# Cross-covariance attention and highway layer: outputs of one batch beside the scores of the next, in a fixed order

## The chip, the core and the metric

The kernel runs on one core of one Trainium2 chip. The metric is the device time of one execution in microseconds (us). Engines: PE multiplies matrices, ACT (ScalarE) applies functions, DVE (VectorE) and POOL (GpSimd) work element by element, SP (SyncE) issues stores; loads that change the type are issued by POOL. Matmul results lie in PSUM, eight banks of 512 f32 per partition, everything else in SBUF.

## What is computed

```python
def _attn_ref(q, k, v, tau):                     # q, k, v: (4, 6336, 256) f32, tau = 1
    qn = q / (np.linalg.norm(q, axis=1, keepdims=True) + 1e-06)
    kn = k / (np.linalg.norm(k, axis=1, keepdims=True) + 1e-06)
    s = kn.transpose(0, 2, 1) @ qn / tau         # 256 x 256 for each batch
    s = s - s.max(-1, keepdims=True)
    a = np.exp(s)
    a /= a.sum(-1, keepdims=True) + 1e-09
    return (v @ a).astype(np.float32)

def _moe_ref(x, w_h, w_t, b_t):                  # x: the 25344 rows of the above
    H = np.maximum(x @ w_h, 0.0)
    T = 1.0 / (1.0 + np.exp(-(x @ w_t + b_t)))
    return (T * H + (1.0 - T) * x).astype(np.float32)
```

## The kernel before

A batch has 6336 rows, 50 tiles of 128 rows (the last has 64). q, k and v are loaded in groups of 16 tiles, cast from f32 to f16 on the way, one row of 256 elements to a partition and tile (`_load_group`, L399 for whole groups, L406 for the short last one). For each of four batches:

- *Scores* (L129, L136, L143): for every tile six matmuls add up k'q and the diagonal blocks of k'k and q'q in two PSUM tiles `sg`. All tiles of a batch must be in before anything is known of the softmax.
- *Chain* (L151 to L248): copies of `sg`, norms from the diagonals, square root on ACT (L172), reciprocal, scaling (L193), exponential (L202), row sums (L204), the attention matrix in f16 in `mr`, its transpose, and its products with w_h and w_t (`ahat`, L241), which are put beside it. `mr` is then the 256 x 768 right side [a | a w_h | a w_t].
- *Outputs*, in pairs of tiles: PE transposes v (L284) into the bank `vtps`; every fourth pair is copied to SBUF by DVE (L296), the others by ACT (L301). Then come the gate matmuls `p3b` (L329) with the bias added by a further matmul (L343), and `p3a` (L336), 512 columns that hold x and x w_h. ACT takes the sigmoid `tt` (L354), DVE max(h, 0) t in `th` (L365) and (t - 1) x in `ux` (L373), a tile at a time, and POOL subtracts (L381). SP stores eight tiles at once (L416).

Loads of the next batch's q and k, and of its first v group, are issued by POOL after the chain (L251), v's other groups from the output loop (L272). Four buffers each hold q and k, three v. The order on each engine is made by the framework's scheduler from this program; it may take PE's work of the next batch forward where its inputs allow. A load waits on a semaphore until its buffer is free; the program has eight semaphores for POOL's loads, used in turn (DMASW0 to DMASW7 in the rows below), and a load that takes one waits until the load that used it last has landed.

## Time and profile before

| | us |
|---|---|
| median of three runs (lowest, highest) | 385.34 (384.37, 387.27) |
| the profiled execution | 384.06 |
| its span | 382.2 |
| PE, DVE, ACT, POOL busy | 296.3, 172.4, 133.2, 186.1 |
| loads in DMA queue 0, share of 16 engines | 76.3% |
| stores in DMA queue 1, share of 16 engines | 22.3% |
| longest pieces of the chain by kind: PE, DMA | 42%, 39% |

The span is the time from the first to the last instruction of the profiled execution. Busy time is summed over it, so an engine that is idle in one stretch and full in the next shows a middling share. GB/s counts bytes as written: a load reads twice as many as it writes. "Idle before <-X" says which work the engine waited for. In the chain, each step is followed back to what released it.

### The profile page before, as it was taken

The numbers are of one execution on the slowest core, as the hardware profiler recorded it, in microseconds if no ns is written. First come the engines' busy times: TensorE is split into PE (matmuls) and PEld (weight loads), VectorE is DVE, ScalarE is ACT, GpSimd is POOL, SyncE is SP. The second block draws the span as 40 slices with busy tenths as digits, with TensorE's granted clock in tenths as the row PEclk, the third lists the DMA queues.
The fourth block names the chain that finished last, engine by engine and source line by source line (L and its number), as shares of the span: only waits on it lengthen the run. The fifth ranks groups of instructions, "written<-read, shape, count | busy, mean of one in ns | idle before, by whom it ended". The sixth has DMA issues, their size and how long they took to land.

```text
span 382.2 us, 6609 instructions
## 1 busy us (share of the span) xinstructions
PE 296.3 (78%) x2637; PEld 211.6 (55%) x2637; DVE 172.4 (45%) x498; ACT 133.2 (35%) x231; POOL 186.1 (49%) x173
## 2 busy tenths in 40 slices
...
GB/s 90 196 198 199 197 198 199 198 210 223 110 157 111 195 237 199 198 198 197 239 250 103 111 163 217 212 200 138 216 231 111 203 237 24 0 101 131 128 194 140
DMA packets 103455, 65.56 MB, mean 172 GB/s; under 512 B 1537, under 2 KB 103425, under 8 KB 103425
## 3 DMA queue, kind: packets, MB, share of 16 engines
q0 software_dynamic: 77568, 39.20, 76.3%
q1 hardware_dynamic: 25856, 25.95, 22.3%
q8 instruction: 20, 0.33, 0.3%
...
## 4 chain that ended last, share of the span: by engine, by line
PE 42%; DMA 39%; DVE 5%; ACT 4%; POOL 4%; issue 3%; POOLq 0%; DVEq 0%; ACTq 0%
DMA k<-in_k_dram 21%; PE p3a L336 19%; DMA v<-in_v_dram 14%; PE p3b L329 8%; DMA q<-in_q_dram 5%; PE p3b L343 4%; PE vtps L284 4%; PE sg L129 3%; ACT tt L354 3%; DVE th L365 2%; DVE ux L373 2%; PE sg L136 2%; PE sg L143 2%; POOL q L399 1%; POOL o L381 1%
## 5 line engine op out<-in xcount | busy, mean ns | idle before, releaser
L381 POOL TENSOR_TENSOR o<-th,ux 128x512 f32<-128x512 f32 (+1 forms) x104 | 128.7, 1246 | 111.1 <-DVE ux L373 93.6
L336 PE MATMUL p3a<-mr,vtsb 128*128 128x512 f16 (+1 forms) x400 | 126.3, 386 | 1.0
L129 PE MATMUL sg<-q,k 128*128 128x256 f16 (+1 forms) x400 | 96.0, 283 | 37.7 <-DMA k<-in_k_dram 35.1
L365 DVE SCALAR_TENSOR_TENSOR th<-p3a,tt 128x256 f32<-128x256 f32 x200 | 84.1, 421 | 41.1 <-ACT tt L354 24.6
L354 ACT ACTIVATE tt<-p3b 128x512 f32<-128x512 f32 (+1 forms) x104 | 60.3, 581 | 101.5 <-PE p3b L343 87.8
L136 PE MATMUL sg<-k 128*128 128x128 f16 (+1 forms) x400 | 90.4, 226 | 0.0
L143 PE MATMUL sg<-q 128*128 128x128 f16 (+1 forms) x400 | 90.2, 226 | 0.0
L329 PE MATMUL p3b<-mr,vtsb 128*128 128x256 f16 (+1 forms) x400 | 87.0, 276 | 0.5 <-ACT tt L354 0.3
L373 DVE SCALAR_TENSOR_TENSOR ux<-tt,p3a 128x256 f32<-128x256 f32 x200 | 82.1, 410 | 0.0
L296 DVE CAST vtsb<-vtps 128x512 f16<-128x512 f32 (+1 forms) x28 | 18.2, 651 | 123.9 <-PE vtps L284 103.7
L284 PE MATMUL vtps<-ident,v 128*128 128x128 f16 (+1 forms) x400 | 45.2, 225 | 29.7 <-DMA v<-in_v_dram 25.4
L129 PEld LDWEIGHTS <-k 128*128 128x128 f16 (+1 forms) x400 | 40.6, 101 | 42.5 <-DMA k<-in_k_dram 41.2
L284 PEld LDWEIGHTS <-v 128*128 128x128 f16 (+1 forms) x400 | 32.4, 101 | 46.9 <-DMA v<-in_v_dram 26.2
L343 PE MATMUL p3b<-btb,ident 128*128 128x256 f16 x200 | 55.3, 277 | 0.0
L301 ACT CAST vtsb<-vtps 128x512 f16<-128x512 f32 (+1 forms) x76 | 43.1, 567 | 33.9 <-PE vtps L284 31.8
L329 PEld LDWEIGHTS <-vtsb 128*128 128x128 f16 (+1 forms) x400 | 38.1, 100 | 22.8 <-issue 2.5
L336 PEld LDWEIGHTS <-vtsb 128*128 128x128 f16 (+1 forms) x400 | 37.5, 99 | 20.0 <-issue 6.3
L143 PEld LDWEIGHTS <-q 128*128 128x128 f16 (+1 forms) x400 | 40.6, 102 | 6.7 <-issue 0.6
L136 PEld LDWEIGHTS <-k 128*128 128x128 f16 (+1 forms) x400 | 40.6, 101 | 1.3 <-issue 0.7
L153 ACT COPY ssb<-sg 128x512 f32<-128x512 f32 x8 | 4.3, 589 | 84.4 <-PE sg L143 84.4
L399 POOL DMA_DIRECT2D k<-in_k_dram x12 | 14.0, 1163 | 27.2 <-PE sg L143 23.5
L343 PEld LDWEIGHTS <-ident 128*128 128x128 f16 x200 | 19.8, 99 | 13.0 <-issue 2.0
...
## 6 DMA issues: line engine op xcount, KB each, us to landing
...
```

What stands on the lines that cost most here:

```text
L129: nc.tensor.matmul(sg[c][:, 0:C], kt_[0:nr, si, bass.ts(c, P)], qt[0:nr, si, :], start=first, stop=False,)
L136: nc.tensor.matmul(sg[c][:, C : C + P], kt_[0:nr, si, bass.ts(c, P)], kt_[0:nr, si, bass.ts(c, P)], start=False, stop=False,)
L143: nc.tensor.matmul(sg[c][:, C + P : C + 2 * P], qt[0:nr, si, bass.ts(c, P)], qt[0:nr, si, bass.ts(c, P)], start=False, stop=last,)
L284: nc.tensor.matmul(vtps[:, u, c, 0:nr], vt_in[0:nr, si + u, bass.ts(c, P)], ident[0:nr, 0:nr], start=(pcnt == 0), stop=(pcnt == 2 * pn - 1),)
L301: nc.scalar.copy(out=vt_sb[:, 0:pn, :, 0 : nrows[0]], in_=vtps[:, 0:pn, :, 0 : nrows[0]],)
L329: nc.tensor.matmul(p3b[0:nr, u, :], vt_sb[:, u, kt, 0:nr], mr[:, kt, 2 * C : 3 * C], start=(kt == 0 and u == 0), stop=False,)
L336: nc.tensor.matmul(pa[0:nr, :], vt_sb[:, u, kt, 0:nr], mr[:, kt, 0 : 2 * C], start=(kt == 0), stop=(kt == 1),)
L343: nc.tensor.matmul(p3b[0:nr, u, :], ident[:, 0:nr], btb, start=False, stop=(u == pn - 1),)
L354: nc.scalar.activation(out=tt[0:nr0, 0:pn, :], in_=p3b[0:nr0, 0:pn, :], func=Act.Sigmoid,)
L365: nc.vector.scalar_tensor_tensor(out=th[0:nr, u, :], in0=p3a[u][0:nr, C : 2 * C], scalar=0.0, in1=tt[0:nr, u, :], op0=AluOp.max, op1=AluOp ...
L373: nc.vector.scalar_tensor_tensor(out=ux[0:nr, u, :], in0=tt[0:nr, u, :], scalar=1.0, in1=p3a[u][0:nr, 0:C], op0=AluOp.subtract, op1=AluOp. ...
L381: nc.gpsimd.tensor_tensor(out=ostg[0:nr0, si : si + pn, :], in0=th[0:nr0, 0:pn, :], in1=ux[0:nr0, 0:pn, :], op=AluOp.subtract,)
```

## The change

The body is written anew for an order that is fixed by the program's text (`manual_schedule`).

- A partition now takes 49 consecutive rows of a batch, so that each load and store moves one contiguous piece per partition; the 64 rows left over are a tile of their own. q and k come in five groups of 12, 12, 12, 9 and 4 tiles with six buffers, v in groups of 16, 16 and 17 with four.
- All scores of batch 0 stand first, then its chain. After that the work goes in 100 slots of two row tiles: gate matmuls, transposes for the slot three ahead, h and x matmuls, the elementwise operations, and as many score tiles of the next batch as `P1_END` says (50 in slots 0 to 17, 50 in 18 to 42, 50 in 43 to 67, none after). The chain of the next batch is spread over seven slots.
- The bias matmuls go; ACT writes the bias into a gate bank two slots ahead (L379), and the gate matmuls add to it.
- `th` and `ux` are formed for two tiles at once (512 elements per partition). h and x of a slot have a bank each out of three (`hx`); the chain's matmuls use the same three. The transposes have one bank (`vT`), emptied by ACT for even and by DVE for odd tiles.
- The square root moves from ACT to POOL as a power, the row sums into the exponential.
- Buffers of loads are refilled from within the slots, one slot after they come free.

The core of the diff; what it removes is the body printed above.

```diff
+    QG = [(0, 12), (12, 12), (24, 12), (36, 9), (45, 4)]
+    NQG = len(QG)
+    QRING = 6
...
+    VG = [(0, 16), (16, 16), (32, 17)]
...
+    VRING = 4
...
+    LOOK = 3
+    P1_END = [18, 43, 68]
...
+    ctx.enter_context(tc.manual_schedule())
...
+    def rows(src2d):
+        return src2d[0:NF, :].rearrange("(p s) c -> p s c", s=NS)
...
+    def load_qk(n):
+        b, g = divmod(n, NQG)
...
+        s0, ns = QG[g]
+        q_t[n] = stream_pool.tile([P, 12, C], f16, tag="q_in", bufs=QRING, name=f"q{n}")
+        k_t[n] = stream_pool.tile([P, 12, C], f16, tag="k_in", bufs=QRING, name=f"k{n}")
+        nc.gpsimd.dma_start(out=q_t[n][:, 0:ns, :], in_=rows(q[b])[:, s0 : s0 + ns, :])
+        nc.gpsimd.dma_start(out=k_t[n][:, 0:ns, :], in_=rows(k[b])[:, s0 : s0 + ns, :])
+        if g == 0:
+            qr_t[b] = stream_pool.tile([P, C], f16, tag="q_rem", bufs=2, name=f"qr{b}")
+            kr_t[b] = stream_pool.tile([P, C], f16, tag="k_rem", bufs=2, name=f"kr{b}")
+            nc.gpsimd.dma_start(out=qr_t[b][0:REM, :], in_=q[b][NF:N, :])
+            nc.gpsimd.dma_start(out=kr_t[b][0:REM, :], in_=k[b][NF:N, :])
...
+    def load_v(m):
...
+        v_t[m] = stream_pool.tile([P, 18, C], f16, tag="v_in", bufs=VRING, name=f"v{m}")
+        nc.gpsimd.dma_start(out=v_t[m][:, 0:ns, :], in_=rows(v[b])[:, s0 : s0 + ns, :])
+        if g == NVG - 1:
+            nc.gpsimd.dma_start(out=v_t[m][0:REM, ns, :], in_=v[b][NF:N, :])
...
+    for n in range(NQG):
+        load_qk(n)
...
-    nc.gpsimd.dma_start(out=bt_sb, in_=moe_b_t.rearrange("(a m) -> a m", a=1))
...
-    btb = const_pool.tile([P, C], f16, tag="btb")
-    nc.scalar.copy(out=btb, in_=btp)
...
+    load_v(0)
+    load_qk(NQG)
...
+    nc.sync.dma_start(out=bt_sb, in_=moe_b_t.rearrange("(a m) -> a m", a=1))
...
+    make_identity(nc, ident0)
...
+    nc.vector.tensor_copy(out=ident, in_=ident0)
+    ones32 = const_pool.tile([P, P], f32, tag="ones32")
+    nc.vector.memset(ones32, 1.0)
...
+    load_v(1)
+    load_v(2)
...
+    def hx_tile(name):
+        return psum_pool.tile([P, 2, C], f32, tag="hx", bufs=3, name=name)
...
+    nc.tensor.matmul(btp[:, 0, :], ones32[0:1, :], bt_sb, start=True, stop=True)
+    btb = const_pool.tile([P, 2, C], f32, tag="btb")
...
+    zbank = []
+    for i in range(2):
+        zb = psum_pool.tile([P, 2, C], f32, tag=f"z{i}", name=f"zbank{i}")
+        nc.tensor.matmul(
+            zb[:, :, :], zeros[:, 0:P], zeros[:, :], start=True, stop=True,
+            skip_group_check=True,
+        )
+        nc.scalar.copy(out=zb[:, :, :], in_=btb[:, :, :])
+        zbank.append(zb)
...
+            kc = kk[0:nr, bass.ts(c, P)]
+            nc.tensor.matmul(
+                S[:, c, :], kc, qq[0:nr, :], start=first and c == 0, stop=last and c == 1
...
+            nc.tensor.matmul(G[:, c, :], kc, kc, start=first and c == 0, stop=False)
+        for c in range(2):
+            qc = qq[0:nr, bass.ts(c, P)]
+            nc.tensor.matmul(G[:, 2 + c, :], qc, qc, start=False, stop=last and c == 1)
...
+        def norms():
...
+            for i in range(4):
+                nc.vector.scalar_tensor_tensor(
+                    out=junk[:, i, :], in0=G[:, i, :], scalar=0.0, in1=ident0,
+                    op0=AluOp.bypass, op1=AluOp.mult, accum_out=n2[:, i : i + 1],
...
+            nc.scalar.copy(out=ssb, in_=S_t.pop(b))
...
+        def invs():
...
+            nc.gpsimd.tensor_tensor(out=nrm, in0=st["n2"], in1=half, op=AluOp.pow)
+            nc.gpsimd.tensor_tensor(out=nrm, in0=nrm, in1=eps, op=AluOp.add)
...
+            nc.vector.reciprocal(out=inv, in_=nrm)
...
+        def pe_cq():
+            cq = hx_tile(f"cq{b}")
+            nc.tensor.matmul(cq[:, 0, :], ones32, st["dcat"][:, :, :], start=True, stop=True)
...
+        def logits():
...
+            nc.vector.tensor_tensor(
+                out=t1, in0=st["ssb"],
+                in1=st["cq"][:, 0:1, :].to_broadcast([P, 2, C]), op=AluOp.mult,
...
+            for c in range(2):
+                nc.scalar.activation(
+                    out=ar[:, c, :], in_=st["t1"][:, c, :], func=Act.Exp,
+                    scale=st["inv"][:, c : c + 1], accum_out=rs[:, c : c + 1],
...
+        def at_copy():
...
+            nc.vector.tensor_copy(out=at_sb, in_=st["at"])
...
+                if ic == 0:
+                    nc.scalar.copy(out=dst, in_=st["ah0"])
+                else:
+                    nc.vector.tensor_copy(out=dst, in_=st["ah1"])
...
+        return [
+            (None, norms),
+            (None, invs),
+            (pe_cq, logits),
+            (None, exps),
+            (None, softmax),
+            (pe_at, at_copy),
+            (both(pe_ahat(0), pe_ahat(1)), both(ahat_copy(0), ahat_copy(1))),
+        ]
...
+    def transpose(t):
...
+        ps = psum_pool.tile([P, 2, 2, P], f32, tag="vT", name=f"vtps{t}")
...
+    def vt_copy(t, ps):
...
+        sb = work_pool.tile([P, 2, 2, P], f16, tag="vTs", bufs=LOOK + 2, name=f"vts{t}")
+        cp = nc.vector.tensor_copy if t % 2 else nc.scalar.copy
...
+    def mains(t, dst, off, seeded):
+        b, i = divmod(t, NPAIR)
+        sb, mr = vT_t[t], mr_t[b]
+        for u, r in enumerate(nrows(i)):
+            for kt in range(2):
+                nc.tensor.matmul(
+                    dst[0:r, u, :], sb[:, u, kt, 0:r], mr[:, kt, off : off + C],
+                    start=(not seeded and kt == 0 and (u == 0 or i == NPAIR - 1)),
+                    stop=(kt == 1 and (u == 1 or i == NPAIR - 1)),
+                    skip_group_check=seeded,
+                )
...
+    def elementwise_ops(t, z, h, x):
...
+        nc.scalar.activation(out=tt, in_=z, func=Act.Sigmoid)
+        if t + 2 < NSLOT:
+            nc.scalar.copy(out=z, in_=btb)
+        th = work_pool.tile([P, 2, C], f32, tag="th", bufs=3, name=f"th{t}")
+        ux = work_pool.tile([P, 2, C], f32, tag="ux", bufs=3, name=f"ux{t}")
...
+                out=th[pr, us, :], in0=h[pr, us, :], scalar=0.0, in1=tt[pr, us, :],
+                op0=AluOp.max, op1=AluOp.mult,
...
+                out=ux[pr, us, :], in0=tt[pr, us, :], scalar=1.0, in1=x[pr, us, :],
+                op0=AluOp.subtract, op1=AluOp.mult,
...
+            nc.gpsimd.tensor_tensor(
+                out=ot[pr, o0 + us.start : o0 + us.stop, :], in0=th[pr, us, :],
...
+    loads_due = []
+    for j in range(NS + 1):
+        p1_tile(0, j)
+        g = group_ended(j)
+        if g is not None:
+            load_qk(g + QRING)
+    load_v(3)
+
+    pend = chain(0)
+    vps = {}
+    for idx, (pe, rest) in enumerate(pend):
+        if pe is not None:
+            pe()
+        rest()
+        if idx < LOOK:
+            vt_copy(idx, transpose(idx))
+
...
+    def p1_target(t):
+        lo = 0
+        for i, e in enumerate(P1_END):
+            if t < e:
+                return i * (NS + 1) + (NS + 1) * (t + 1 - lo) // (e - lo)
+            lo = e
+        return total1
...
+    for t in range(NSLOT):
+        b, i = divmod(t, NPAIR)
+        due, loads_due = loads_due, []
+        pe_part, rest_part = chain_q.pop(0) if chain_q else (None, None)
+        z = zbank[t % 2]
+        mains(t, z, 2 * C, True)
+        ps = transpose(t + LOOK) if t + LOOK < NSLOT else None
+        if pe_part is not None:
+            pe_part()
+        h = hx_tile(f"h{t}")
+        mains(t, h, C, False)
+        x = hx_tile(f"x{t}")
+        mains(t, x, 0, False)
+        if rest_part is not None:
+            rest_part()
+        elementwise_ops(t, z, h, x)
+        if ps is not None:
+            vt_copy(t + LOOK, ps)
...
+                    loads_due.append((load_v, bb * NVG + g + VRING))
+        for fn, arg in due:
+            fn(arg)
+        while done1 < p1_target(t):
+            pb, j = divmod(done1, NS + 1)
+            p1_tile(pb + 1, j)
+            g = group_ended(j)
+            if g is not None:
+                loads_due.append((load_qk, (pb + 1) * NQG + g + QRING))
+            if j == NS:
+                chain_q += chain(pb + 1)
+            done1 += 1
+        vT_t.pop(t)
```

Three places show how work moved on the engines. The first is POOL's queue between the loads and the first work of the outputs. Before, with q and k of batch 1 (`q_1_464` to `k_3_473`) and v's second group (`v_1_480`):

```order
L399 DMA q_1_464<-in_q_dram 128x16x256 [waits DMASW0_49,PE_49]
L399 DMA k_1_465<-in_k_dram 128x16x256 [waits DMASW1_49]
L399 DMA q_2_468<-in_q_dram 128x16x256 [waits DMASW2_49,PE_49]
L399 DMA k_2_469<-in_k_dram 128x16x256 [waits DMASW3_49]
L406 DMA q_3_472<-in_q_dram 128x256 [waits DMASW4_49,PE_49]
L406 DMA q_3_472<-in_q_dram 64x256 [waits DMASW5_49]
L406 DMA k_3_473<-in_k_dram 128x256 [waits DMASW6_49]
L406 DMA k_3_473<-in_k_dram 64x256 [waits DMASW7_49]
L399 DMA v_0_478<-in_v_dram 128x16x256 [waits DMASW0_49]
L399 DMA v_1_480<-in_v_dram 128x16x256 [waits DMASW1_49]
L381 TENSOR_TENSOR o_0_482<-th_0_0_519,ux_0_0_520 128x512 [waits DVE_49]
```

Now, from the loads of batch 1 on (`q_371`: its fourth group, `q_457`: batch 2, `v_465`: v of batch 1):

```order
L82 DMA q_371<-in_q_dram 128x2304 [waits DMASW2_49,PE_49]
L83 DMA k_372<-in_k_dram 128x2304 [waits DMASW3_49]
L82 DMA q_429<-in_q_dram 128x1024 [waits DMASW4_49,PE_49]
L83 DMA k_430<-in_k_dram 128x1024 [waits DMASW5_49]
L82 DMA q_457<-in_q_dram 128x3072 [waits DMASW6_49,PE_49]
L83 DMA k_458<-in_k_dram 128x3072 [waits DMASW7_49]
L87 DMA qr_461<-in_q_dram 64x256 [waits DMASW0_49]
L88 DMA kr_462<-in_k_dram 64x256 [waits DMASW1_49]
L96 DMA v_465<-in_v_dram 128x4096 [waits DMASW2_49]
L206 TENSOR_TENSOR nrm_482<-n_0_468,half 128x4 [waits DVE_49]
L207 TENSOR_TENSOR nrm_482<-nrm_482,eps 128x4 [waits Pool_49]
L398 TENSOR_TENSOR o_558<-th_554,ux_555 128x512 [waits DVE_49]
```

The two small operations on `nrm`, which were not on POOL, stand behind all these loads and ahead of the first subtraction.

The second place is DVE in the first pairs of batch 0. Before (`th`, `ux` for one tile each):

```order
L296 CAST vtsb_0_8_560<-vtps_0_8_555 128x512 [waits PE_49]
L365 SCALAR_TENSOR_TENSOR th_0_0_519<-p3a_0_505,tt_0_0_517 128x256 [waits Activation_49]
L373 SCALAR_TENSOR_TENSOR ux_0_0_520<-tt_0_0_517,p3a_0_505 128x256
L365 SCALAR_TENSOR_TENSOR th_0_0_519<-p3a_1_511,tt_0_0_517 128x256
L373 SCALAR_TENSOR_TENSOR ux_0_0_520<-tt_0_0_517,p3a_1_511 128x256
L365 SCALAR_TENSOR_TENSOR th_0_2_548<-p3a_2_534,tt_0_2_546 128x256 [waits Activation_49]
L373 SCALAR_TENSOR_TENSOR ux_0_2_549<-tt_0_2_546,p3a_2_534 128x256
L365 SCALAR_TENSOR_TENSOR th_0_2_548<-p3a_3_540,tt_0_2_546 128x256 [waits PE_49]
```

Now:

```order
L286 CAST mr_514<-ah_1_527 128x512 [waits PE_49]
L387 SCALAR_TENSOR_TENSOR th_554<-h_541,tt_551 128x512 [waits PE_49,Activation_49]
L392 SCALAR_TENSOR_TENSOR ux_555<-tt_551,x_546 128x512 [waits PE_49]
L339 CAST vts_560<-vtps_536 128x512
L387 SCALAR_TENSOR_TENSOR th_598<-h_585,tt_595 128x512 [waits PE_49,Activation_49]
L392 SCALAR_TENSOR_TENSOR ux_599<-tt_595,x_590 128x512 [waits PE_49]
L387 SCALAR_TENSOR_TENSOR th_645<-h_632,tt_642 128x512 [waits PE_49,Activation_49]
L392 SCALAR_TENSOR_TENSOR ux_646<-tt_642,x_637 128x512 [waits PE_49]
L339 CAST vts_650<-vtps_627 128x512
```

`th` and `ux` are one operation each for two tiles, and the copy of transposed v (`vts`) stands behind them in every second slot.

The third place is PE in these pairs, equal rows left out. Before, around a transposition:

```order
L329 MATMUL p3b_0_6_591<-mr_415,vtsb_0_6_531 128x256
L343 LDWEIGHTS ident
L343 MATMUL p3b_0_6_591<-btb,ident 128x256
L284 LDWEIGHTS v_0_108
L284 MATMUL vtps_0_12_613<-ident,v_0_108 128x128 [waits Activation_49]
L336 LDWEIGHTS vtsb_0_4_502
L336 MATMUL p3a_5_569<-mr_415,vtsb_0_4_502 128x512 [waits DVE_49]
```

Now, in slot 1, from the gate matmuls (`zbank`) over h and x to the scores of batch 1 (`S`, `G`):

```order
L347 LDWEIGHTS vts_495
L347 MATMUL zbank_136<-mr_514,vts_495 128x256
L324 LDWEIGHTS v_96 [waits DVE_49]
L324 MATMUL vtps_580<-ident,v_96 128x128 [waits PE_49]
L347 MATMUL h_585<-mr_514,vts_495 128x256
L347 MATMUL x_590<-mr_514,vts_495 128x256 [waits PE_49]
L169 LDWEIGHTS k_99
L169 MATMUL S_562<-q_98,k_99 128x256
L172 MATMUL G_563<-k_99 128x128
L175 MATMUL G_563<-q_98 128x128
```

The bias matmul is gone, and the transposes stand between the gate and the h matmuls of the same slot. In every second slot they wait for DVE, in the others for ACT. One more wait lies at the start: the identity is now made by POOL behind the loads of batch 0 and of the first group of batch 1, DVE converts it before it sets its ones, and PE's first matmul (the bias, spread over the partitions) waits for these.

## Rows read from the trace of the kernel before

**Rows 1.** The page: span, busy us of each engine, bytes moved in 40 equal slices, and packets.

```profile
span 382.2 us, 6609 instructions
...
PE 296.3 (78%) x2637; PEld 211.6 (55%) x2637; DVE 172.4 (45%) x498; ACT 133.2 (35%) x231; POOL 186.1 (49%) x173
...
GB/s 90 196 198 199 197 198 199 198 210 223 110 157 111 195 237 199 198 198 197 239 250 103 111 163 217 212 200 138 216 231 111 203 237 24 0 101 131 128 194 140
DMA packets 103455, 65.56 MB, mean 172 GB/s; under 512 B 1537, under 2 KB 103425, under 8 KB 103425
```

**Rows 2.** The chain of waits in order of time: start us, us, what.

```profile
41.47 25.93 DMA k<-in_k_dram
67.69 25.49 DMA v<-in_v_dram
...
328.58 0.85 PE p3a L336 x2
```

**Rows 3.** Windows: stretch, us, busy us of PE, PEld, DVE, ACT, POOL, PEclk, DMA share, GB/s.

```profile
0.00:10.00 10.00, 0.37 (x1) 0.10 (x1) 0.30 (x2) 1.95 (x3) 9.04 (x15) 1.00 0.78 95
...
40.00:48.00 8.00, 8.00 (x108) 7.39 (x107) 0.00 (x0) 0.11 (x1) 2.70 (x3) 1.00 1.46 199
```

**Rows 4.** Timeline of POOL, start: start us, us, engine, line, work [idle before <-releaser].

```profile
1.28 0.88 POOL L71 DMA_DIRECT2D wht<-in_moe_w_h_dram  x1 [0.34 <-issue]
...
3.73 1.19 POOL L399 DMA_DIRECT2D q<-in_q_dram  x1
...
18.90 0.53 POOL L406 DMA_DIRECT2D k<-in_k_dram  x1 [4.93 <-DMA k<-in_k_dram]
...
67.69 1.15 POOL L399 DMA_DIRECT2D v<-in_v_dram  x1 [3.96 <-DMA k<-in_k_dram]
```

**Rows 5.** Timeline of DVE and ACT in the chain of batch 0.

```profile
60.86 0.18 DVE L174 RECIPROCAL inv<-nrt 128x4 f32<-128x4 f32 x1 [10.89 <-ACT nrt L172]
...
62.43 0.88 DVE L193 SCALAR_TENSOR_TENSOR t<-ssb,inv,cqbs 128x256 f32<-128x256 f32 x2 [0.87 <-ACT cqbs L189]
...
62.90 1.28 ACT L202 ACT_TABLE_LOAD   x1
...
64.86 0.69 DVE L204 TENSOR_REDUCE rs<-araw 128x2 f32<-128x512 f32 x1 [1.55 <-ACT araw L202]
...
68.08 1.07 ACT L248 CAST mr<-ahat 128x512 f16<-128x512 f32 x2 [0.64 <-PE ahat L241]
```

**Rows 6.** Timeline: a wide copy of DVE, and one pair of batch 3.

```profile
48.44 0.69 DVE L296 CAST vtsb<-vtps 128x512 f16<-128x512 f32 x1 [47.31 <-PE vtps L284]
...
49.05 0.28 DVE L162 SCALAR_TENSOR_TENSOR junk<-ssb,ident 128x128 f32<-128x128 f32 x1
...
344.46 0.38 PE L329 MATMUL p3b<-mr,vtsb 128*128 128x256 f16 x2
...
344.68 0.27 PE L343 MATMUL p3b<-btb,ident 128*128 128x256 f16 x1
...
345.04 0.60 ACT L354 ACTIVATE tt<-p3b 128x512 f32<-128x512 f32 x1 [0.28 <-PE p3b L343]
...
345.74 0.42 DVE L365 SCALAR_TENSOR_TENSOR th<-p3a,tt 128x256 f32<-128x256 f32 x1 [0.27 <-ACT tt L354]
...
346.08 0.41 DVE L373 SCALAR_TENSOR_TENSOR ux<-tt,p3a 128x256 f32<-128x256 f32 x1
...
347.21 0.39 PE L284 MATMUL vtps<-ident,v 128*128 128x128 f16 x4
```

**Rows 7.** Groups of instructions by form: line, work, count | busy us, mean ns | idle.

```profile
L381 POOL TENSOR_TENSOR o<-th,ux 128x512 f32<-128x512 f32 x96 | 123.1, 1290 | 111.0 <-DVE ux L373 93.6 <-issue 16.8
L354 ACT ACTIVATE tt<-p3b 128x512 f32<-128x512 f32 x96 | 57.4, 598 | 97.8 <-PE p3b L343 84.1 <-ACT vtsb L301 6.4 <-DVE ux L373 4.9
L381 POOL TENSOR_TENSOR o<-th,ux 128x256 f32<-128x256 f32 x4 | 2.9, 719 | 0.0
```

**Rows 8.** Timeline of PE at the end of batch 3.

```profile
374.36 0.59 PE L336 MATMUL p3a<-mr,vtsb 128*64 128x512 f16 x2
```

More of the change, by code (lines that the diff above doesn't have):

```diff
@@ new lines @@
+    eps = const_pool.tile([P, 4], f32, tag="eps")
+    nc.vector.memset(eps, 1e-6)
+    zeros = const_pool.tile([P, 2 * C], f16, tag="zeros")
+    nc.vector.memset(zeros.bitcast(u16), 0)
+    load_v(1)
+    load_v(2)
+    def hx_tile(name):
+        return psum_pool.tile([P, 2, C], f32, tag="hx", bufs=3, name=name)
+    btp = hx_tile("btp")
+    nc.tensor.matmul(btp[:, 0, :], ones32[0:1, :], bt_sb, start=True, stop=True)
+    btb = const_pool.tile([P, 2, C], f32, tag="btb")
+    for u in range(2):
+        nc.scalar.copy(out=btb[:, u, :], in_=btp[:, 0, :])
@@ new lines, with v_of, nrows @@
+    vT_t = {}
+    o_t = {}
+    NSLOT = B * NPAIR
+    def v_of(b, s):
+        g = max(i for i in range(NVG) if VG[i][0] <= s)
+        return v_t[b * NVG + g], s - VG[g][0]
+    def nrows(i):
+        return [P, REM] if i == NPAIR - 1 else [P, P]
+    def transpose(t):
+        b, i = divmod(t, NPAIR)
+        vt, s = v_of(b, 2 * i)
+        ps = psum_pool.tile([P, 2, 2, P], f32, tag="vT", name=f"vtps{t}")
+        nr = nrows(i)
+        for u in range(2):
+            for c in range(2):
+                nc.tensor.matmul(
+                    ps[:, u, c, 0 : nr[u]], vt[0 : nr[u], s + u, bass.ts(c, P)],
+                    ident[0 : nr[u], 0 : nr[u]],
+                    start=(u == 0 and c == 0), stop=(u == 1 and c == 1),
+                )
+        return ps
```

485 lines of the change are left out of this document (150 added, 335 removed).

## The prediction

> **What bounds the kernel now.** I read the page first. PE, the busiest engine, works 78% of the span, and GB/s alternates between a plateau of 195 to 199 and slices of 0 to 140 [rows 1]. So no single engine is the limit: stretches that wait for loads alternate with stretches that wait for PE. The chain of waits, read next, shows where: two of its longest pieces are loads, k to 67.4 us and v to 93.2 us [rows 2]. The v tile of batch 0 stood in POOL's queue behind all q and k of batch 1. In the last batch nothing is loaded any more, and 25 pairs of row tiles run from 328.58 to 374.95, 1.85 us each [rows 2, 8]. Third, POOL's own rows: POOL issues a load only when an older one has landed, and sits idle for it 4.93 and 3.96 us [rows 4]. By the order of waits there are eight load semaphores, so each load waits for the eighth before it. Whatever stands behind such an issue in POOL's queue waits too.
>
> **The change, part by part.** All times are of the profiled execution, whose span is 382.2 us.
>
> *Start.* q is now the first work on POOL; before, it came at 3.73, behind a chain that began at 1.28 [rows 4]. The first window moved 95 GB/s of 198 over 10 us [rows 3], 4.8 us of flow, so the flow began at 5.2, 1.5 us after q's issue. In the new kernel it begins at about 2.8.
>
> *The new wait.* The square roots of the norms move from ACT to POOL (`nrm`, two operations), and stand behind 35 loads. The last of these, v of batch 1, waits for semaphore lane 2, which the load `q_371` of batch 1 (nine tiles) signals. Up to that load stand all q and k of batch 0 (6.49 MB as written), the weights (0.26), v of batch 0 (3.24), and of batch 1 both remainders, three groups of q and k and the q half of the fourth (5.38): 15.37 MB. At 198 GB/s [rows 1] that is 77.6 us, so v is issued at 80.4 and POOL is free at 81.6. Behind it wait the whole softmax chain of batch 0 and with it every slot. The two operations on 128x4 cost between nothing and 0.72 each (the 128x256 row of POOL [rows 7]); I take 0.5, nearer the small end but not launch-free: 82.6.
>
> The identity also stands behind loads now (the remainder k of batch 1 waits for q's last group), and PE's first matmul waits for VectorE, which waits for it. So the scores of batch 0 begin at about 36 us instead of running with the loads. They are 50 tiles of 0.44 us (18 tiles in the 8.00 us of a full window [rows 3]): 22 us, to about 60 with a slow first clock. I cost this at nothing, since POOL's gate at 82.6 covers it. With the cover gone it would be the start.
>
> *The chain of batch 0.* Before, 8.3 us from the reciprocal (60.86) to the end of the last copy into `mr` (69.15). Less 0.9 for the table load that `araw` waits for, 0.7 for the sum that the exponential now carries, 0.5 for two copies that go to two engines [rows 5]: 6.2. The sigmoid's table load (1.28) sticks out by 0.6. Slots begin at 82.6 + 6.2 + 0.6 = 89.4.
>
> *A slot.* PE issues matmuls of 256 columns every 0.11 us (the second of the two in 0.38 ends 0.11 after the first's 0.27), four of 128 in 0.22 [rows 6]: gates 0.44, transposes 0.22, h 0.44, x 0.44. Bias matmuls, two of 0.11, are gone, about 22 us of PE over 100 slots, which counts only where PE sets the pace. It does not: the transposes of the next slot need the single vT bank, which VectorE empties after both wide operations. From an even slot's start: last gate matmul 0.33 + 0.27, 0.09 to ACT, sigmoid 0.60, 0.10 to VectorE [rows 6]: the first wide operation starts at 1.39. A 128x512 operation has no row here except the cast: 0.69 long, the next one starts 0.61 after it [rows 6]. Two narrow ones, unpipelined, are 0.84; pipelined, 0.68. I take 0.61, a wide row being nearest. Then the cast starts at 2.61, ends at 3.30, and PE, one more such hop later, may transpose at 3.38.
> - Slots 18 to 67, two score tiles: length 2.42, PE is there at 2.86 and waits 0.52. The odd slot's copy is ACT's and ready in time. A pair takes 5.36, a slot 2.68; 50 slots 134.0.
> - Slots 0 to 17, 2.78 score tiles: length 2.76, PE arrives at 3.20 and waits 0.18: 2.85 a slot, 51.3.
> - Slots 68 to 99, no scores: length 1.54, PE arrives at 1.98 and waits 1.40: 4.48 a pair, 2.24 a slot, 71.7. That is more than the 1.85 of before.
>
> *What else lies in a slot.* ACT gains the seed, a write into PSUM that no row shows: between 0 and the 0.60 of the sigmoid [rows 7]. With 0.60 ACT has 1.5 of 2.24 us, hidden behind the wait on vT. POOL has 1.29 [rows 7] and 31 load issues of up to 1.19 [rows 4], 1.8 of 2.68, also hidden; three buffers of `th` and `ux` cover a hold of two slots. From 89 us on the DMA must still move about 20 MB of loads (101 us) and up to slot 68 17.8 MB of stores (45 to 90 us, at 396 or 198 GB/s), in 195 us: hidden too.
>
> *Chains of batches 1 to 3* lie in seven slots each. Two table loads and the exponentials put the sigmoid 2.6 us late, the roots queue behind POOL's subtraction (1.6), three more wide VectorE operations cost 1.8, PE's extra matmuls 1.5. Odd slots have slack, so of 7.5 I take 5.5 (bounds 3 and 7.5): 16.5 for three.
>
> *End.* From the last matmul (374.95) to the end 7.3 us [rows 1, 8], by the same steps.
>
> Sum: 89.4 + 51.3 + 134.0 + 71.7 + 16.5 + 7.3 = 370.2 us of span. The profiled execution took 384.06 for its span of 382.2 (+1.9), and the median of the three runs, 385.34, lies 0.3% above (+1.2): **373 us**, 3% faster. The overlap is worth much more by itself; a late start and a slower last batch eat most of it.
>
> **The rivals.**
> 1. *The loads flow faster.* Each partition now reads 9 to 17 KB in one piece; all packets of before are under 2 KB [rows 1], so no row has this case. The flow lies between 198 (no change) and the 250 GB/s of the best mixed slice [rows 1]. At 212, a quarter of the way, the gate comes after 72.5 instead of 77.6 us: 368. Against it: the plateau is flat to 1%, and may belong to the memory and not to the packet. The Trainium skill, DMA: Bandwidth & Descriptors, "Why small descriptors are slow", says for it that every packet costs about three cycles beside one per 32 bytes; for 1 KB packets that is some 9%, and by this estimate the gate would come 6 to 7 us sooner and the time would be about 367. No row of before shows it.
> 2. *The gate does not hold* (the roots run before the loads have landed). Then the scores of batch 0 are the start: 60, the norms and the chain 8.5, slots at 68.5 instead of 89.4: 352. Against it: POOL's idle rows [rows 4].
> 3. *Slower: VectorE's wide operations.* Place: the two in front of the cast in every even slot. At the price of two unpipelined narrow ones (0.84 instead of 0.61) each pair of slots grows by 0.46, 50 pairs by 23 us: 396. Every 0.1 us per pair is 5 us. It decides from 0.17 per pair on (0.69 each: no longer 1% faster), and from 0.32 on (0.77) the change is slower than before. For it: 0.42 and 0.41 for half the width [rows 6]; against it: the cast's 0.69 for the same width.
>
> **How the numbers follow.** Forecast 0.50 (own range 366 to 381), faster loads 0.16, no gate 0.06: together 0.72 for faster by over 1%, that is under 381.5 (1% is about what a measurement of this kernel can tell from no change). The wide operations hold 0.28: 0.16 up to 389.2 (within 1%), 0.12 beyond (slower). The range 357 to 388 leaves out the no-gate case (0.06) and the slower end (0.13). It takes in the bounds of the chains (minus 7, plus 6), of the roots (1) and of the flow.
>
> **What would show it.** Right: POOL idle on DMA until about 80 us with `nrm` (L206) at about 82; first sigmoid near 90; PE's transposes (L324) waiting for VectorE's cast (L339) in every second slot; slots of 2.85, 2.68 and 2.24 us; PE idle for some 22 us between 60 and 85. Wrong: first sigmoid before 75 or after 97; wide operations (L387, L392) starting more than 0.69 apart; waits of POOL on DMA within the slots that stop VectorE; a granted clock below full in the last 32 slots, where PE works 69% of the time.

## The result, and the profile after

The changed kernel takes 372.08 us (median of 4 runs, 371.74 to 372.20) beside 385.76 for the kernel before (4 runs): a ratio of 0.9643, interval 0.9605 to 0.9681. The profiled execution took 372.11 us, its span 369.9. Forecast were 373 and 370.2.

First the page of the kernel after; its columns are those of [rows 1].

```profile
span 369.9 us, 6923 instructions
...
PE 271.1 (73%) x2844; PEld 226.2 (61%) x2844; DVE 178.2 (48%) x333; ACT 164.8 (45%) x286; POOL 170.6 (46%) x184
...
PE   0001996017999998889999978999999677777781
...
PEclk9999999555999999899999999999999989999997
...
GB/s 133 213 214 212 213 216 214 211 214 217 20 143 215 261 265 264 240 226 240 214 204 295 199 223 119 114 136 153 191 113 223 39 93 135 116 113 116 113 115 135
DMA packets 13377, 65.58 MB, mean 177 GB/s; under 512 B 1569, under 2 KB 3618, under 8 KB 8738
```

PE does 25 us less work than before, and the alternation of [rows 1] is gone: one long stretch at the start in which the DMA is full and PE idle but for batch 0's scores (slices 0 to 9, 92 us), then one in which PE works nearly without a gap, and the last batch, in which it works some 70 to 80% of the time. The load plateau stands at 211 to 217 GB/s, not at 198, with an eighth of the packets.

POOL's timeline shows the start, in the columns of [rows 4].

```profile
1.23 0.73 POOL L82 DMA_DIRECT2D q<-in_q_dram  x1 [0.79 <-POOLq L485]
...
35.00 0.29 POOL masks.py:199 TENSOR_SCALAR_AFFINE_SELECT ident<-ident 128x128 f32<-128x128 f32 x1
...
45.23 0.56 POOL L82 DMA_DIRECT2D q<-in_q_dram  x1 [7.90 <-PE G L175]
...
77.22 0.56 POOL L96 DMA_DIRECT2D v<-in_v_dram  x1 [2.29 <-DMA q<-in_q_dram]
77.81 1.06 POOL L206 TENSOR_TENSOR nrm<-n,half 128x4 f32<-128x4 f32 x1
78.94 0.20 POOL L207 TENSOR_TENSOR nrm<-nrm,eps 128x4 f32<-128x4 f32 x1
```

The roots follow the last load at once: the gate is there, 3.2 us sooner than forecast. Not all of POOL's idle time ahead of it is a wait for the DMA: between 37 and 60 us it waits four times, 19.4 us in all, until PE has scored a group whose buffer the next load needs (the row at 45.23). The timeline of all engines goes on with the chain of batch 0, which answers [rows 5], up to the first sigmoid:

```profile
79.18 0.18 DVE L209 RECIPROCAL inv<-nrm 128x4 f32<-128x4 f32 x1 [16.93 <-POOL nrm L207]
...
83.83 0.76 PE L258 MATMUL at<-ident,mr 128*128 128x128 f16 x4 [2.25 <-DVE mr L248]
...
85.38 1.89 PE L273 MATMUL ah<-wht,at_sb 128*128 128x512 f16 x4 [0.79 <-DVE at_sb L266]
...
87.30 0.69 DVE L286 CAST mr<-ah 128x512 f16<-128x512 f32 x1 [1.98 <-PE ah L273]
...
88.93 1.28 ACT L377 ACT_TABLE_LOAD   x1 [1.89 <-PE zbank L347]
90.22 0.60 ACT L377 ACTIVATE tt<-zbank 128x512 f32<-128x512 f32 x1
```

And one pair of slots of the last batch, which answers [rows 6]:

```profile
329.80 0.69 DVE L387 SCALAR_TENSOR_TENSOR th<-h,tt 128x512 f32<-128x512 f32 x1 [0.25 <-PE h L347]
330.41 0.68 DVE L392 SCALAR_TENSOR_TENSOR ux<-tt,x 128x512 f32<-128x512 f32 x1
...
331.01 0.68 DVE L339 CAST vts<-vtps 128x512 f16<-128x512 f32 x1
...
331.75 0.40 PE L324 MATMUL vtps<-ident,v 128*128 128x128 f16 x4 [1.21 <-DVE vts L339]
...
333.29 0.39 PE L324 MATMUL vtps<-ident,v 128*128 128x128 f16 x4
```

VectorE's operations start 0.61 and 0.60 apart, and PE's transposes wait 1.21 us for the cast behind them, in every second slot only. (A granted clock below full in the last 32 slots, named as a sign of being wrong, did not come: it is 0.98 in 290 to 362 us.) By the starts of the 100 sigmoids (90.22 the first, 360.37 the last), against the forecast:

| | forecast | measured |
|---|---|---|
| last load of the start issued | 80.4 | 77.22 |
| roots done | 82.6 | 79.14 |
| chain of batch 0, `inv` to the last copy | 6.2 | 8.81 |
| first sigmoid (slots begin + 0.7) | 90.1 | 90.22 |
| slots 0 to 17, each | 2.85 | 2.84 |
| slots 18 to 67, a pair | 5.36 | 5.33 (2.42 and 2.91) |
| slots 68 to 95, a pair | 4.48 | 4.45 (1.53 and 2.92) |
| slots 96 to 99, to the last matmul | 8.96 | 6.56 |
| chains of batches 1, 2, 3, beyond the slots' own time | 5.5 each | 6.3, 5.7, 6.7 |
| last matmul to the end | 7.3 | 8.3 |

### The profile page after: what moved, and what is told of

Read it like the earlier page. It is cut to its first block, busy times and chain, and to the rows that moved or that the text cites. A ratio compares the mean times of both kernels' runs of the same rounds, so it can differ in the third digit from the quotient of the medians.

```text
span 369.9 us, 6923 instructions
## 1 busy us (share of the span) xinstructions
PE 271.1 (73%) x2844; PEld 226.2 (61%) x2844; DVE 178.2 (48%) x333; ACT 164.8 (45%) x286; POOL 170.6 (46%) x184
## 4 chain that ended last, share of the span: by engine, by line
PE 46%; DVE 19%; DMA 14%; issue 9%; POOL 6%; ACT 3%; DVEq 0%; POOLq 0%; ACTq 0%
DMA q<-in_q_dram 11%; PE h L347 10%; DVE ux L392 8%; PE S L169 8%; PE vtps L324 7%; PE zbank L347 6%; PE x L347 6%; DVE vts L339 6%; PE G L172 4%; PE G L175 4%; POOL o L398 3%; DVE th L387 3%; DMA k<-in_k_dram 3%; PE ah L273 1%; POOL nrm L206 1%
## 5 line engine op out<-in xcount | busy, mean ns | idle before, releaser
L398 POOL TENSOR_TENSOR o<-th,ux 128x512 f32<-128x512 f32 x96 | 123.8, 1291 | 127.4 <-DVE ux L392 106.0
L347 PEld LDWEIGHTS <-vts 128*128 128x128 f16 x1200 | 110.5, 99 | 17.5 <-issue 6.3
L387 DVE SCALAR_TENSOR_TENSOR th<-h,tt 128x512 f32<-128x512 f32 (+1 forms) x104 | 69.3, 669 | 83.9 <-PE h L347 55.3
L169 PE MATMUL S<-q,k 128*128 128x256 f16 x392 | 87.0, 276 | 0.0
L172 PE MATMUL G<-k 128*128 128x128 f16 x392 | 76.1, 221 | 0.0
L392 DVE SCALAR_TENSOR_TENSOR ux<-tt,x 128x512 f32<-128x512 f32 (+1 forms) x104 | 67.9, 656 | 0.1
L324 PE MATMUL vtps<-ident,v 128*128 128x128 f16 (+1 forms) x400 | 40.0, 222 | 30.9 <-DVE vts L339 27.8
L347 PE MATMUL zbank<-mr,vts 128*128 128x256 f16 (+1 forms) x400 | 61.5, 276 | 0.6 <-DVE mr L286 0.6
L347 PE MATMUL x<-mr,vts 128*128 128x256 f16 (+1 forms) x400 | 61.7, 277 | 0.0
L347 PE MATMUL h<-mr,vts 128*128 128x256 f16 (+1 forms) x400 | 61.4, 276 | 0.0
L379 ACT COPY zbank<-btb 128x512 f32<-128x512 f32 x98 | 57.8, 590 | 3.1
L169 PEld LDWEIGHTS <-k 128*128 128x128 f16 x392 | 38.7, 99 | 4.1 <-issue 0.6
L172 PEld LDWEIGHTS <-k 128*128 128x128 f16 x392 | 38.8, 99 | 0.8
L82 POOL DMA_DIRECT2D q<-in_q_dram x20 | 11.4, 568 | 29.2 <-PE G L175 19.4
```

What stands on the lines that cost most here:

```text
L82: nc.gpsimd.dma_start(out=q_t[n][:, 0:ns, :], in_=rows(q[b])[:, s0 : s0 + ns, :])
L169: nc.tensor.matmul(S[:, c, :], kc, qq[0:nr, :], start=first and c == 0, stop=last and c == 1)
L172: nc.tensor.matmul(G[:, c, :], kc, kc, start=first and c == 0, stop=False)
L324: nc.tensor.matmul(ps[:, u, c, 0 : nr[u]], vt[0 : nr[u], s + u, bass.ts(c, P)], ident[0 : nr[u], 0 : nr[u]], start=(u == 0 and c == 0), st ...
L347: nc.tensor.matmul(dst[0:r, u, :], sb[:, u, kt, 0:r], mr[:, kt, off : off + C], start=(not seeded and kt == 0 and (u == 0 or i == NPAIR - 1)),
L379: nc.scalar.copy(out=z, in_=btb)
```

## The experiments

Times are medians; the changed kernel's 372.08 is the one to compare with. In the text "slot" lengths are the distances between sigmoids. The runs are numbered e1 to e11, as the expectations name them.

**The gate at the start.** Two things hold batch 0 back in the changed kernel, each covered by the other if the prediction is right. The first run (e1) moves the five last loads behind the roots.

```diff
-        if g is not None:
+        if g is not None and g + QRING < 2 * NQG:
             load_qk(g + QRING)
-    load_v(3)
...
         rest()
+        if idx == 1:
+            load_qk(2 * NQG)
+            load_v(3)
```

> One edit in the changed kernel: the five loads that stand last ahead of the roots on POOL (q, k and both remainders of batch 2's first group, v of batch 1) are issued behind the roots of batch 0. Theory (the roots' place in POOL's queue holds the start): the scores of batch 0 end at 61.1 as in the trace of the changed kernel, the roots (1.3 us there) at 63, the chain takes the same 8.8 us, and the first sigmoid comes at 75 instead of 90.2. POOL is still held by its loads until about 77, which three buffers of th and ux cover. 372 - 15 = 357, between 354 and 360. Rival (the loads themselves are the limit, the roots only stood where the data would have been late anyway): slots that begin sooner wait for q, k or v, and the time stays between 367 and 372.

356.29 us (355.79 to 356.87). POOL's timeline:

```profile
62.96 1.04 POOL L206 TENSOR_TENSOR nrm<-n,half 128x4 f32<-128x4 f32 x1 [1.47 <-DVE junk L196]
...
77.33 0.57 POOL L96 DMA_DIRECT2D v<-in_v_dram  x1 [2.26 <-DMA q<-in_q_dram]
77.92 1.28 POOL L398 TENSOR_TENSOR o<-th,ux 128x512 f32<-128x512 f32 x1
```

The last load goes out when it did (77.33), but the roots run 14 us ahead of it, the first sigmoid comes at 74.72, and nearly every later slot has its old length. The wait was one of position in a queue, not of data. The second run (e2) makes the identity first, alone:

```diff
+    ident0 = const_pool.tile([P, P], f32, tag="ident0")
+    make_identity(nc, ident0)
     for n in range(NQG):
         load_qk(n)
```

> One edit in the changed kernel: the identity matrix is made on POOL ahead of the first load, so that PE scores batch 0 while it is loaded. Theory (the late scores are covered by POOL's gate): the scores end near 37 instead of 61, POOL no longer waits for PE at four load issues (19.4 us there), but the last load's lane still waits for the same bytes at the same flow, and the first sigmoid stays at 90 within 1.5 us: 372, between 370 and 374. Rival (the late scores hold the start, since POOL's loads wait for them): the first sigmoid comes up to 16 us sooner, 356 to 368.

372.04 us (370.31 to 373.10): nothing. The scores now lie under the loads (PE busy 23.02 of the 28 us from 10 to 38) and end at 39.6 instead of 61.3, and yet, in POOL's timeline:

```profile
78.08 0.56 POOL L96 DMA_DIRECT2D v<-in_v_dram  x1 [2.29 <-DMA q<-in_q_dram]
78.66 1.05 POOL L206 TENSOR_TENSOR nrm<-n,half 128x4 f32<-128x4 f32 x1
```

So the 22 us by which the scores were late are hidden whole by the gate. The third run (e3) does both, and puts the loads of batch 1 and later into a list from which each slot issues one group.

```diff
+            load_v(1)
+            load_qk(6)
...
+        fifo += due
+        for fn, arg in fifo[:1]:
             fn(arg)
+        fifo = fifo[1:]
```

> Both edits at once in the changed kernel, and the loads of batch 1 behind the first group moved behind the roots, one load group per slot. Theory (two covers, each hiding the other): scores end near 37, roots near 39, chain 8.8, first sigmoid near 49 to 51, some 40 us sooner; 372 - 40 = 332. From there on 10.5 MB fewer have landed when the slots begin, and 7.2 MB more must come within the first 17 slots (46 us, 156 GB/s of the 213 that the plateau shows, beside 4 MB of stores), so up to 12 us may come back: 330 to 345. Rival (the loads are the limit of the start): above 355.

357.40 us (356.97 to 358.52): the gate is gone (first sigmoid at 53.64, against 49 to 51 expected), but most of the gain is given back. POOL's timeline, and one row of DVE's waits (us in total, times, longest):

```profile
77.55 0.53 POOL L83 DMA_DIRECT2D k<-in_k_dram  x1 [5.58 <-DMA v<-in_v_dram]
...
96.81 0.53 POOL L83 DMA_DIRECT2D k<-in_k_dram  x1 [4.73 <-DMA q<-in_q_dram]
...
131.55 1.06 POOL L203 TENSOR_TENSOR nrm<-n,half 128x4 f32<-128x4 f32 x1
```

```profile
DVE inv L206 <- POOL nrm L204: 24.4, 4, 18.2
```

One group per slot is more than the DMA takes away. POOL stands at its loads again, slots 10, 11 and 14 stretch to 3.5, 4.9 and 7.7 us, and slot 20 lasts 20.9 (6.9 in the changed kernel), since VectorE waits up to 18.2 us for roots that stand behind loads. It is the same gate at a second place. Of the expectation, the early start held, and the claim that at most 12 us would come back fell: 25 did. The time lies where the rival had it, but the start, which that rival held to be limited by the loads, came 37 us sooner; the last runs show what the order of the same loads is worth.

**The vT bank** (e4). In slots whose copy is VectorE's, the copy goes ahead of the wide operations.

```diff
+        ahead = ps is not None and (t + LOOK) % 2 == 1
+        if ahead:
+            vt_copy(t + LOOK, ps)
         if rest_part is not None:
             rest_part()
         elementwise_ops(t, z, h, x)
         if ps is not None:
-            vt_copy(t + LOOK, ps)
+            if not ahead:
+                vt_copy(t + LOOK, ps)
```

> One edit in the changed kernel: in the slots in which VectorE empties the vT bank it does so ahead of its two wide operations instead of behind them. Theory (the bank's release behind the wide operations is what lengthens every second slot): pairs of slots fall from 5.33 to 4.84 us (both slots at PE's 2.42) between the chains, by 0.2 in the first 18, and in the last batch from 4.45 to 3.6, where the copy on ACT, behind sigmoid and seed, comes late next: 12 + 2 + 13 = 27 us less, 345 (341 to 350). Rival (the pace of the slots is set by PE's and VectorE's work or by the loads, and the wait moves elsewhere): 362 to 372.

346.58 us (345.93 to 347.25). All slots of the middle stage are 2.42 (PE's own length), the last batch's pairs 3.51. PE's waits for vT, first of the changed kernel and then of this run:

```profile
PE vtps L324 <- DVE vts L339: 27.8, 37, 2.3
```

```profile
PE vtps L324 <- ACT vts L339: 3.9, 12, 0.8
```

The 27.8 us are gone, and what is late next is the copy on ACT, as expected. The single bank, emptied last in VectorE's slot, cost the change 25.5 us, nearly twice its whole gain.

**The flow** (e5). q and k are loaded with the row order of the kernel before.

```diff
+    def rows_sp(src2d):
+        return src2d[0:NF, :].rearrange("(s p) c -> p s c", p=P)
-        nc.gpsimd.dma_start(out=q_t[n][:, 0:ns, :], in_=rows(q[b])[:, s0 : s0 + ns, :])
+        nc.gpsimd.dma_start(out=q_t[n][:, 0:ns, :], in_=rows_sp(q[b])[:, s0 : s0 + ns, :])
```

> One edit in the changed kernel: q and k are loaded with the row order of the kernel before (row s*128+p to partition p, so that each piece is one row) instead of 9 to 17 KB in one piece for each partition; the scores sum over all rows, so the order doesn't matter to them. Theory (the longer pieces raised the flow from 198 to 213 GB/s): the plateau falls back to 196 to 200, one load issue on POOL costs about 1.15 us as before instead of 0.55, the last load of the start is issued at 81 to 83 instead of 77.2, and the time is 376 to 378. Rival (the flow rose for another reason, such as the missing gap at the start or the tile order): plateau 211 to 217, time 371 to 373.

375.86 us (374.81 to 377.07). The window 18 to 34 us, when only q, k, the weights and the first v load; columns as in [rows 3]; first the changed kernel, then this run, then two of its POOL rows:

```profile
18.00:34.00 16.00, 0.00 (x0) 0.00 (x0) 0.00 (x0) 0.00 (x0) 2.85 (x5) 1.00 1.05 211
```

```profile
18.00:34.00 16.00, 0.00 (x0) 0.00 (x0) 0.00 (x0) 0.00 (x0) 3.58 (x5) 1.00 1.46 198
```

```profile
2.47 1.04 POOL L86 DMA_DIRECT2D k<-in_k_dram  x1
...
82.39 0.57 POOL L99 DMA_DIRECT2D v<-in_v_dram  x1 [2.46 <-DMA q<-in_q_dram]
```

The flow falls to 198, the gate moves from 77.22 to 82.39, and the first sigmoid to 95.41. So the length of the pieces of q and k made the difference, and it was worth 5.2 us at the gate and 3.8 in the time. (The last sigmoid is 5.6 us later, 366.01 beside 360.37. Behind the issue of the last store, which the edit doesn't touch, 3.5 us pass in this run and 5.3 in the changed kernel; no run says why.) That is the mechanism of rival 1. The Trainium skill, DMA: Bandwidth & Descriptors, "Why small descriptors are slow", charges every packet a fixed cost; the prediction's estimate from it, some 9% for 1 KB pieces and 6 to 7 us, stands beside the measured 7% and, with v still in long pieces, 5.2 us.

**The seed** (e6). The bias comes back as two matmuls at the start of each slot, and ACT's seed goes.

```diff
-        if t + 2 < NSLOT:
-            nc.scalar.copy(out=z, in_=btb)
+        bias(z)
         mains(t, z, 2 * C, True)
...
+            nc.tensor.matmul(
+                z[:, u, :], ones16, bt16, start=(u == 0), stop=False,
```

> One edit in the changed kernel: the bias is added by two matmuls of 256 columns at the start of each slot again, and ACT's seed of the gate bank is left out. Theory (by the slot's steps, the vT bank sets the pair of slots, so only the bias matmuls of the even slot lengthen it): 0.22 us for each pair, 0.11 a slot, 11 us over 100 slots: 383 (380 to 386). Rival 1 (PE sets the pace of every slot): 0.22 a slot, 394. Rival 2 (ACT's seed costs as much as it saves): 370 to 375.

395.27 us (394.63 to 396.01), as rival 1's number had it, but not for its reason: the long slots of the middle stage stayed at 2.91 and the short ones grew from 2.42 to 2.84, by 0.42 instead of 0.22. PE's timeline:

```profile
213.77 0.39 PE L360 MATMUL zbank<-bt,ones 1*128 1x256 f16 x2
214.09 0.61 PE L351 MATMUL zbank<-mr,vts 128*128 128x256 f16 x4
214.59 0.40 PE L328 MATMUL vtps<-ident,v 128*128 128x128 f16 x4
```

The two matmuls of one row hold the gates back by 0.32, and the gates take 0.50 to the transposes instead of 0.44. This was the edit's own form, so it was run again (e7) in the form of the kernel before: weights `ident`, moved 128 rows of bias.

```diff
-                z[:, u, :], ones16, bt16, start=(u == 0), stop=False,
+                z[:, u, :], ident, bt16, start=(u == 0), stop=False,
```

> As e6, but with the bias matmuls in the form of the kernel before (weights: the 128x128 identity; moved: the bias broadcast to 128 rows, f16), since e6's matmuls of one row took PE 0.42 us a slot instead of 0.22. Theory (the vT bank sets the pair, the slots where PE waits for it hide the bias): the short slot grows from 2.42 to 2.64, the long one stays at 2.91, 0.11 a slot on average in the middle stage and 11 us over all: 383 (381 to 386). Rival (each slot grows by 0.22): 394.

382.11 us (381.58 to 383.61): short slots of 2.64 and long ones of 2.91 in the middle stage, as worked out. In PE's timeline the gates now follow after 0.22:

```profile
216.94 0.38 PE L358 MATMUL zbank<-bt,ident 128*128 128x256 f16 x2
217.16 0.60 PE L349 MATMUL zbank<-mr,vts 128*128 128x256 f16 x4
217.59 0.39 PE L326 MATMUL vtps<-ident,v 128*128 128x128 f16 x4
```

Without the seed the change would have been worth 3 us (ratio 0.9901, 0.9864 to 0.9938).

**The chains.** For batches 1 and 2 (e10) the loads due are issued behind the roots instead of ahead.

```diff
-        due, loads_due = loads_due, []
+        due = []
+        if not chain_q or len(chain_q) < 6:
+            due, loads_due = loads_due, []
```

> One edit in the changed kernel: the loads that fall due while a chain's first two steps run are issued on POOL behind the roots instead of ahead of them. Theory (in the chains of batches 1 and 2 the roots stand behind four load issues of 0.53 to 0.58 us, and PE waits 2.13 us for what follows them): 2.1 us less for each of two chains, 368 (366.5 to 369.5). Rival (the tables and VectorE's extra operations alone set the chain's cost): 371 to 373.

369.94 us (368.79 to 370.11): 2.1 less, half of what was expected. In batch 1's chain the roots start at 144.88 instead of 146.81, PE no longer waits 2.13 us for what follows them, and its eight slots take 25.4 us instead of 27.6. POOL's rows, first of the changed kernel and then of this run:

```profile
146.81 1.06 POOL L206 TENSOR_TENSOR nrm<-n,half 128x4 f32<-128x4 f32 x1
```

```profile
144.88 1.04 POOL L206 TENSOR_TENSOR nrm<-n,half 128x4 f32<-128x4 f32 x1
```

Batch 2's chain kept its length: there POOL had issued its loads before the roots already, and they stood only behind a subtraction. The first was read from rows, and the second wrongly taken to be like it. In the time alone 2 us is little beside the spread of four runs of one kernel (2.8 us in e2); the rows carry this reading and the next one.

For batch 0 (e11), matmuls of zeros fill PE's idle time ahead of and in the chain.

```diff
+    warm(76, "warm0")
     pend = chain(0)
...
+        if idx == 2:
+            warm(8, "warm1")
```

> One edit in the changed kernel: 84 matmuls of 512 columns of zeros, whose result nobody reads, fill PE's idle time in the softmax chain of batch 0 (76 between the end of the scores at 61 and the roots, 8 behind the chain's first transposes). Theory (the chain of batch 0 took 8.8 us instead of the forecast 6.2 mostly because PE had stood still for 18 us and its granted clock was 0.50 in 79 to 90): its matmuls fall to the times that the same ones have at full clock in batch 1's chain (1.22 to 0.65, 0.76 to 0.39, 1.89 to 1.03), the chain to about 7.0 us, the first sigmoid to 88.5, and the time to 370.3 (369.5 to 371). Rival (VectorE, ACT and the hops set the chain's length): chain 8.5 to 8.8, time 371.5 to 373.

370.15 us (369.50 to 371.02). The windows of the changed kernel, then of this run, in the columns of [rows 3], and two of this run's matmuls:

```profile
61.00:79.00 18.00, 0.88 (x12) 0.58 (x10) 0.93 (x8) 1.07 (x2) 3.78 (x8) 0.59 1.04 213
79.00:90.00 11.00, 6.46 (x27) 3.55 (x28) 4.11 (x10) 3.23 (x7) 0.14 (x1) 0.50 1.09 217
```

```profile
61.00:79.00 18.00, 17.80 (x97) 8.68 (x95) 0.93 (x8) 0.75 (x2) 3.93 (x8) 1.00 1.04 213
79.00:90.00 11.00, 7.89 (x43) 4.19 (x43) 4.24 (x11) 4.62 (x10) 0.73 (x2) 0.85 1.08 215
```

```profile
83.87 0.60 PE L258 MATMUL at<-ident,mr 128*128 128x128 f16 x4 [0.56 <-DVE mr L248]
85.26 1.04 PE L273 MATMUL ah<-wht,at_sb 128*128 128x512 f16 x4 [0.79 <-DVE at_sb L266]
```

With PE busy through 61 to 79 the clock granted in the chain is 0.85 instead of 0.50 (the lower of its two levels, 1.2 GHz). `ah` takes 1.04 instead of 1.89 and the chain 7.17 us (79.85 to 87.02) instead of 8.81. So 1.6 of the 2.6 us by which the chain was mis-sized were PE's clock. (The first sigmoid comes at 89.25, only 1.0 sooner, because in this run the last load was issued 0.7 later.)

The long wait ahead is the smaller part of it. In e1 PE was busy with scores until 61.9 us and the chain began at 64.3, with the granted clock still full. PE's rows there:

```profile
65.05 0.70 PE L220 MATMUL cq<-dcat,ones 128*128 128x256 f32 x2 [1.78 <-DVE dcat L212]
...
68.32 0.77 PE L258 MATMUL at<-ident,mr 128*128 128x128 f16 x4 [2.29 <-DVE mr L248]
...
69.88 1.89 PE L273 MATMUL ah<-wht,at_sb 128*128 128x512 f16 x4 [0.79 <-DVE at_sb L266]
```

`cq` runs at full speed (1.22 in the changed kernel), `at` and `ah` take as long as there, and the chain takes 8.19 us (64.30 to 72.49): the granted clock is 1.00 until 66, 0.52 in 66 to 67 and 0.50 from there to 75. PE had no work from 63.3 to 65.0, 0.95 us of it in 65 to 66 and 0.03 in 66 to 68. By these three chains (8.81, 8.19, 7.17) some 0.6 us go with the long wait, and 1.0 with short idle times of PE just ahead of the chain and within it; the two sets of zero matmuls were not run apart.

**All together** (e8). Identity first, early roots, the copies of vT ahead (ACT's between sigmoid and seed), the sigmoid's table loaded in batch 0's chain, and the later loads spread over the slots by a list.

```diff
+    LOADS = {
+        0: [(Q, 7)], 1: [(K, 7)], 3: [(V, 2)], 4: [(Q, 8)], 6: [(K, 8)], 8: [(Q, 9)],
...
+        for fn, arg in LOADS.get(t, []):
+            fn(arg)
```

> The changed kernel with e2, e4 and early roots together, ACT's copy of vT between sigmoid and seed, the sigmoid's table loaded in batch 0's chain, and all loads of batch 1 and later spread over the slots one transfer at a time (none in the slots of a chain's roots), because in e3 POOL stood at its loads' lanes up to 5.6 us and batch 1's roots came 16 us late behind them. Theory (all the gains are in series): first sigmoid near 50, 18 slots of 2.73, 50 of 2.42 with 5 us for each of two chains, 32 of 1.6 with 5, and 9.5 at the end: 50 + 49 + 131 + 56 + 9.5 + 2 = 298 (292 to 308). Rival (the DMA, which then has 57 MB to move in 230 us, 248 GB/s where 250 to 270 is the most that a slice of e1 or e4 shows with loads and stores mixed): slots wait for loads, 310 to 330.

313.88 us (312.93 to 314.65): 16 us above the forecast and outside its range, inside the rival's. The slots have the lengths worked out (2.42, and 1.53 in the last batch), but the chains' slots do not; slots 18 and 43 take 7.54 and 8.59. PE's waits name the reason:

```profile
PE S L175 <- DMA kr<-in_k_dram: 16.9, 3, 8.3
```

Of these 16.9 us, 8.3 are the wait at the very start; the two in slots 18 and 43 are 3.9 and 4.6, not 8.3 each, as the next expectation has it. The last run (e9) issues the remainders and the next batch's first groups earlier, v mostly later; the lines of the list are e8's and then e9's.

```diff
-        0: [(Q, 7)], 1: [(K, 7)], 3: [(V, 2)], 4: [(Q, 8)], 6: [(K, 8)], 8: [(Q, 9)],
-        9: [(K, 9)], 11: [(V, 3)], 12: [(Q, 10)], 14: [(K, 10)], 15: [(R, 2)], 16: [(Q, 11)],
...
+        0: [(Q, 7)], 1: [(K, 7)], 3: [(V, 2)], 4: [(Q, 8)], 6: [(K, 8), (R, 2)], 8: [(Q, 9)],
+        9: [(K, 9)], 10: [(Q, 10)], 12: [(K, 10)], 14: [(V, 3)], 16: [(Q, 11)],
...
```

> As e8, with the loads of the next batch's remainders and first q and k groups issued earlier and v's later: in e8 PE waited 8.3 us each for the remainder kr at the start of batch 1's and batch 2's scoring (slots 18 and 43), where the load had been issued 10 us ahead behind others. Theory (the place of these loads in the order, not the flow, cost that time): both waits go, the two slots fall from 7.5 and 8.6 to 5 or less, 314 - 7 = 307 (304 to 310). Rival (the DMA is the limit there, the same bytes are late anyway): 312 to 315.

303.71 us (302.23 to 304.46), a ratio of 0.7854 (0.7822 to 0.7885), just under the range: slots 18 and 43 fall to 3.32 and 2.62, 10 us in all. The same row, and the page:

```profile
PE S L175 <- DMA kr<-in_k_dram: 8.3, 1, 8.3
```

```profile
span 300.9 us, 6917 instructions
...
PE 268.2 (89%) x2844; PEld 231.2 (77%) x2844; DVE 176.4 (59%) x333; ACT 157.3 (52%) x287; POOL 168.2 (56%) x184
```

Of these waits only the one at the very start is left, and the rival, that the DMA is the limit, falls: the same bytes come in time in another order. Little is left of the DMA either: in 52 to 198 us it moves 243 GB/s while PE is busy for 144 of 146 us.

## Why the prediction was right, point by point

- **The gate** held as described: five loads moved out of its way are worth 15.8 us, and the late scores below it nothing. That POOL waited for PE, and not for the DMA, through 19.4 us of the stretch ahead changed nothing: with the scores early (e2) the last load goes out at 78.08. The time of 352 that rival 2 gave for a start without it was met within 5 us by the run with the roots ahead.
- **The flow** was too low. It was taken from [rows 1] as 198, and 213 came, by rival 1's mechanism (with pieces of 4 to 17 KB, not 9 to 17: the groups of four tiles are shorter); the price of a load issue (1.19 in [rows 4]) fell to 0.55 with it. At 213 the 15.37 MB take 72.2 us instead of 77.6. The issue came 3.2 us sooner, not 5.4: by the first slice (133 of 213 over 9.25 us) the flow began at 3.5 instead of 2.8, and the remaining 1.5 us no row explains.
- **The roots** took 1.06 for the power and 0.20 for the sum on 128x4, 1.33 in all with the gaps, where 1.0 was taken. In all that is inside the bounds (0 to 1.44), but the power alone is beyond the 0.72 that was the most for one. POOL's 128x256 subtraction is no upper bound for another operation.
- **The chain of batch 0** took 8.81 instead of 6.2, 1.6 of it PE's clock; the other 1.0 was not taken apart. The forecast named PE's 22 idle us and did not price what they, and the short idle times in the chain, do to the work behind them. The table load stuck out by its full 1.28, not by 0.6. Together with the roots this ate the 3.2 us of the faster flow, and so the first sigmoid came at 90.22 against 90.1: a right number from errors of opposite sign.
- **The slots** came out within 0.03 us a pair in the middle and the last stage. The price taken for VectorE's wide operations (0.61) was that of the cast's row [rows 6], a choice of the nearest row that 5 us for each 0.1 us per pair hung on; it measured 0.60 to 0.61, and rival 3's 0.84 did not occur. The run with the cast ahead shows that the wait named was the cause.
- **The bias matmuls**: that they count "only where PE sets the pace. It does not" was too strong. PE does set it in the slots between two VectorE copies and in nearly all of slots 0 to 17 (2.86 becomes 3.08 in e7), and putting the matmuls back in place of the seed costs 10.0 us. The sum held because the slot lengths had been worked out without them.
- **The chains of batches 1 to 3** cost 18.7 in place of 16.5, inside the bounds. One part is shown: loads ahead of batch 1's roots, 2.1 us. The rest (table loads, VectorE behind `inv`) was not taken apart.
- **The last slots.** The forecast charged slots 96 to 99 as two full pairs, 8.96. They took 6.56: the last three transpose nothing for a later slot. These 2.4 us hid the 2.2 by which the chains were dearer, and the 1.0 that the stretch behind the last matmul took beyond 7.3 went against the slots' 1.2. The gate and the slots held by their mechanism; that the span came out within 0.3 us (369.9 beside 370.2) was luck.
